# A chunked delta-rule attention ahead of two expert stages: state kept block-diagonal, keys and queries no longer spread, batch and token on the partitions, eight heads in one group

## The chip, the cores and the metric

The kernel runs on one core of a Trainium2 chip. The metric is the time of the device in microseconds for one execution; several runs give a median, and one further execution was recorded by the profiler. Five engines work side by side and meet through semaphores: TensorE (PE, matrix products into PSUM), VectorE (DVE), ScalarE (ACT), GpSimd (POOL) and SyncE (SP), which here issues DMAs. Each of them goes through its own instructions in order.

## The reference

Attention over 4 batches, 8 heads, 768 tokens and a head dimension of 48. Each head of each batch has a state of 48x48 that is carried from token to token:

```python
k_n = k / (np.linalg.norm(k, axis=-1, keepdims=True) + 1e-06)
for t in range(S):
    y[:, :, t] = np.einsum('bhd,bhde->bhe', q[:, :, t], state)
    v_old = np.einsum('bhde,bhd->bhe', state, kt)
    state = state + bt[:, :, :, None] * np.einsum('bhd,bhe->bhde', kt, vt - v_old)
```

Here kt, vt and bt are the normalised key, the value and beta of token t. The output, 3072 rows (batch and token) of 384, goes through a mixture of 8 experts of which each row takes the one with the highest logit, and the result through a second one of 4 experts that all rows pass, weighted by given probabilities. An expert is relu(x w1) w2 with 1024 hidden columns.

## The kernel before

**Attention in chunks.** 768 tokens are 24 steps of 32 tokens, `st = 4*c + s`, with six chunks c of four steps s. A step treats 32 tokens of 4 batches and 8 heads at once: 32 (batch, head) pairs. Within a step the recurrence is solved with a triangular matrix of 32x32 for each pair. `gram` (L311) multiplies keys with keys and with queries into G and Pm; `inverse` (L337) turns G into the inverse of the triangular matrix, all 32 x 4 matrices of a chunk at once: a transpose (L344), 31 columns, each with a product and a sum on DVE (L356, L357), and a transpose back (L380). The result goes as high and low fp16 halves into TPd, and by DMA (`stage_t`, L390) into the block-diagonal tiles TP of two steps each.

**A step.** `inject` (L406) puts v into a PSUM bank; `chain` (L411) subtracts state times keys (L424), writes the rest r as a high fp16 half on ACT and a low half on DVE, multiplies it with TP (L432) into u, again a high half (ACT) and a low half (DVE, L436), and adds keys times u to the state in PSUM (L444), whose two halves S go back to SBUF (ACT, and DVE L449) for the next step. Every product of two such numbers takes three matmuls (high-high, high-low, low-high). `outputs` (L453) computes the output from queries and state (L461) and from u and TP (L467); ACT copies it to ys, and the router's `done` (L539 on) normalises it, computes the expert logits and stores the rows (xr to xd). ACT's operations of this kind come from one helper and have its line, L203; DVE's and POOL's products of two tensors have L206.

**The form of the operands.** The tile kq holds the transposed keys and queries of a chunk (`keys`, L261: normalise, split, DMA transpose from l2, which lies in wa). It holds two (batch, head) pairs over its 128 partitions, 64 for each, and `spread` (L297) copies the keys (KT; DVE, some ACT) and queries (QT, ACT) of each step into zero-padded tiles, so that one matmul of 128 rows treats two pairs without mixing them. `stage_k` (L386) transposes the spread keys by DMA into kb for the state update. The eight heads are two groups g of four, with PSUM banks cp of their own, and each step runs chain and outputs for either.

**What sets the order.** Class `Plan` is a list scheduler: every operation is added with an assumed duration, the keys it reads and writes, and a priority; the plan starts the ready operation with the lowest priority on each engine, operations of `chain` being urgent, and emits all engines' instructions in the resulting order. `OFF` is a table of about 100 offsets to the priorities, by tag. SyncE issues the DMAs in order; a DMA also waits for the eighth one before it. Idle stretches of TensorE are filled with matmuls on zeros (L195). At the end of the attention `weights` loads the first experts' weights into the tiles kq, wa and wb. The first expert matmul is at L800.

## Time and profile before

| what | value |
|---|---|
| runs | 1446.67, 1441.14, 1443.97 us, median 1443.97 |
| profiled execution | 1452.08 us, span 1450.5 us |
| busy over the span | PE 89%, DVE 64%, ACT 48%, POOL 49% |
| chain that ended last, by engine | PE 50%, DVE 13%, DMA 11%, issue 11% |
| attention, to the first expert matmul | 472.05 us |

The shares of the whole span mix two different parts: the attention in the first third and the two expert stages behind it. Busy times of the attention alone are in the windows below. "Idle before" in a group of instructions is time in which the engine stood still just before one of them, and the name behind the arrow is what ended it.

### The profile page before, as it was taken

What the parts mean: (1) busy time and instruction counts of PE and PEld (TensorE: products, weight loads), DVE (VectorE), ACT (ScalarE), POOL (GpSimd) and SP (SyncE); (2) the same over time, 40 slices, a digit from 0 to 9 for tenths busy, and PEclk for the clock granted to TensorE, in tenths of its full rate; (3) what the DMA queues carried; (4) which work ended last, traced back from release to release, by engine and by line L of the source; (5) the groups of instructions that cost most, each with busy time, mean ns of one, the idle gap of its engine ahead of it and who ended that gap; (6) DMA issues with size and microseconds to landing.
All of it is one profiled execution on the core that took longest, in us unless ns stands there. A gap on an engine that the chain in (4) does not pass through costs nothing.

```text
span 1450.5 us, 35997 instructions
## 1 busy us (share of the span) xinstructions
PE 1289.6 (89%) x14904; PEld 1066.8 (74%) x14904; DVE 930.2 (64%) x1877; ACT 690.9 (48%) x1348; POOL 714.4 (49%) x927
## 2 busy tenths in 40 slices
PE   7677686777778798899989999999999999999997
PEld 4355475665566654455679999899998999999997
DVE  7979888859745556653285556855578555564654
ACT  2846464645464444542254444544445444444433
POOL 3445554533223478310185445744468444456664
PEclk8688878868889999999999999999999999999999
DMA  8968988794797786763220102101121011011200
GB/s 124 184 94 159 109 132 113 124 128 84 123 116 128 190 226 173 211 177 101 74 63 23 45 23 87 46 23 35 33 77 34 23 34 34 23 36 54 66 34 34
DMA packets 358888, 130.48 MB, mean 90 GB/s; under 512 B 314688, under 2 KB 348992, under 8 KB 358720
## 3 DMA queue, kind: packets, MB, share of 16 engines
q1 hardware_dynamic: 351856, 112.69, 40.4%
q0 software_dynamic: 6864, 15.45, 3.3%
q8 instruction: 118, 1.93, 0.6%
q14 instruction: 50, 0.41, 0.1%
HBM read 76.38 MB, written 14.96 MB: 63 GB/s over the span
## 4 chain that ended last, share of the span: by engine, by line
PE 50%; DVE 13%; DMA 11%; issue 11%; SPq 5%; POOL 5%; ACT 4%; another core or an unknown queue 0%; POOLq 0%; ACTq 0%; DVEq 0%
PE b L928 23%; PE b L947 20%; SPq L215 4%; DMA s<-in_moe_w_dram 4%; DMA TP<-TPd 4%; DVE tmp L356 2%; DMA kq<-wa 2%; PE b L800 1%; POOL q L775 1%; DVE KT L306 1%; POOL S L936 1%; DVE X L357 1%; DVE wa L357 1%; PE Sp L444 1%; DVE v L753 1%
## 5 line engine op out<-in xcount | busy, mean ns | idle before, releaser
L928 PE MATMUL b<-wb,v 128*128 128x256 f16 x3456 | 392.8, 273 | 0.3 <-ACT a L930 0.2
L928 PEld LDWEIGHTS <-v 128*128 128x128 f16 x3456 | 336.7, 98 | 37.9 <-issue 0.9
L947 PE MATMUL b<-v,h 128*128 128x192 f16 x4032 | 353.5, 247 | 11.6 <-DVE cc L955 6.4
L947 PEld LDWEIGHTS <-h 128*128 128x128 f16 x4032 | 338.7, 98 | 16.6 <-issue 8.6
L936 POOL TENSOR_TENSOR S<-a 128x256 f32<-128x256 f32 x192 | 149.7, 800 | 272.7 <-ACT a L930 272.5
L940 DVE TENSOR_TENSOR h<-a,h 128x768 f16<-128x768 f32 x96 | 135.0, 1407 | 145.8 <-ACT h L939 138.3
L940 DVE TENSOR_TENSOR h<-S,h 128x1024 f16<-128x1024 f32 x96 | 120.9, 1259 | 125.6 <-ACT h L939 125.6
L939 ACT ACTIVATE h<-S 128x1024 f16<-128x1024 f32 x96 | 101.4, 1056 | 199.5 <-POOL S L936 179.8
L930 ACT ACTIVATE a<-b 128x512 f32<-128x512 f32 x192 | 113.4, 594 | 143.8 <-PE b L928 134.8
L936 POOL TENSOR_TENSOR S<-S,a 128x256 f32<-128x256 f32 x96 | 133.8, 1394 | 0.0
L195 PE MATMUL wp<-wz 128*128 128x512 f16 x304 | 85.4, 424 | 10.1 <-DVE LG L556 7.4
L939 ACT ACTIVATE h<-a 128x768 f16<-128x768 f32 x96 | 80.8, 842 | 2.8
L936 POOL TENSOR_TENSOR S<-a,S 128x256 f32<-128x256 f32 x96 | 73.7, 768 | 7.2
L195 PEld LDWEIGHTS <-wz 128*128 128x128 f16 x398 | 40.6, 107 | 47.0 <-issue 18.0
L203 ACT ACTIVATE QT<-kq 64x512 f16<-64x512 f16 x96 | 60.0, 626 | 11.4 <-PE cp L461 6.5
L815 POOL DMA_DIRECT2D x<-y x27 | 19.7, 733 | 90.5 <-DVE y L813 80.8
L432 PE MATMUL cp<-r,TP 128*128 128x48 f16 x576 | 31.4, 198 | 36.8 <-DMA TP<-TPd 20.6
L803 DVE SCALAR_TENSOR_TENSOR h<-b,h 128x432 f16<-128x432 f32 (+2 forms) x72 | 39.6, 552 | 36.2 <-ACT h L802 35.3
L444 PE MATMUL Sp<-u,kb 64*128 64x48 f16 x1152 | 35.4, 193 | 29.4 <-DVE S L449 15.2
L955 DVE TENSOR_TENSOR cc<-b,sm 128x192 f32<-128x192 f32 x192 | 58.5, 345 | 3.1 <-ACT sm L952 3.1
L753 DVE SCALAR_TENSOR_TENSOR v<-s,v 128x512 f16<-128x512 f32 (+2 forms) x56 | 45.5, 840 | 23.0 <-ACT v L752 21.1
L550 POOL TENSOR_TENSOR ys<-ys,sc 128x384 f32<-128x384 f32 x24 | 20.9, 871 | 79.7 <-ACT xr L203 36.0
(249 smaller groups left out, 2145.6 us busy)
## 6 DMA issues: line engine op xcount, KB each, us to landing
wb<-x SPq DMA_DIRECT2D x72, 256.0 KB
...
```

Of the source, the lines that this page charges most:

```text
L195: nc.tensor.matmul(out=out,lhsT=wz[:,0:128],rhs=wz[:,0:out.shape[1]],start=start,stop=True,skip_group_check=True)
L203: self.op('A',dur,lambda: self.nc.scalar.activation(out=out,in_=in_,func=func,scale=scale),reads,writes,tag,**k)
L215: self.op(q,occ,(lambda: e.dma_start_transpose(out=out,in_=in_)) if turn else (lambda: e.dma_start(out=out,in_=in_)),reads,list(writes)+[( ...
L444: for a,b in ps: nc.tensor.matmul(out=Sp[:,pp,u],lhsT=kb[R,a,u],rhs=u16[R,b,u-o],start=(st,u,a,b)==(0,0,0,0),stop=last and b==1,skip_group ...
L753: self.op('V',69+1.042*n,lambda: self.nc.vector.scalar_tensor_tensor(out=lo,in0=s,scalar=64.0,in1=hi,op0=ALU.mult,op1=ALU.subtract),reads+ ...
L928: for c,y in PASS: nc.tensor.matmul(out=F[k][:,f],lhsT=w[:,c,d,c_:c_+128],rhs=self.xk[B%2][d][:,y,256*i:256*i+256],start=(f,z)==(0,0),stop ...
L930: self.op('A',620,lambda k=k,g=g: A.activation(out=a[ja][:,g].rearrange("p x t -> p (x t)"),in_=F[k].rearrange("p a t -> p (a t)"),func=AF ...
L936: self.op('G',750,lambda o=o,x=x,y=y,w=w: G.tensor_tensor(out=X[o],in0=X[x],in1=X[y],op=w),ka,[ks])
L939: self.op('A',200+.833*m,lambda h=h,q=q,g=g: A.activation(out=h[:,0,:,q],in_=g,func=AF.Copy),kg,[kh+(0,)])
L940: self.op('V',200+1.042*m,lambda h=h,q=q,g=g: V.tensor_tensor(out=h[:,1,:,q],in0=g,in1=h[:,0,:,q],op=ALU.subtract),kg+[kh+(0,)],[kh+(1,)])
L947: for z,(c,d) in enumerate(PASS): nc.tensor.matmul(out=Q[k][:,o,0:192],lhsT=h[:,c,g,x],rhs=w[:,d,m,y],start=(m,o,z)==(0,0,0),stop=(m,z)==( ...
L955: self.op('V',340,lambda o=o,k=k,y=y,x=x: V.tensor_tensor(out=o,in0=Q[k][:,y,0:192],in1=s[:,x],op=ALU.add),[('Q',k),('sm',z,x)],[ko])
```

## The change

The diff keeps the algorithm, its precision (high and low halves) and the expert stages, and lays out the attention in another way.

* k and q are no longer spread: the tiles KT and QT, `spread`, `stage_k`, `stage_q` and the DMA transposes into kb are gone. In their place the state is kept block-diagonal in S16, `[128, 2, 4, 4, 2, 48]`, zeroed once by POOL, and the products with it (`by_state`) are matmuls of 32 stationary columns, one for each batch, with 96 moving columns.
* The partition is batch and token. k and q are loaded in pieces of 32 tokens of one batch and 8 heads, 16 DMAs each for a chunk where there were 4 (8 of another shape for the first chunk); the first chunk's q comes over ACT's queue. l2k and l2q are tiles of their own, and kqT and l2k exist three times. The state update takes the keys straight from l2k, in matmuls of 32 rows, into four PSUM banks.
* The eight heads are one group: one bank c0 for v, r and the output, one bank c1 for u; r, u and the output are 128x384, S's halves 64x768 (two for each step and half).
* The gram's matmuls are 64 rows by 32 columns with 64 moving columns.
* `OFF` is empty, so priorities are those of the code. wa and wb are halves of one tile wab, the weights' claims stand in another order, NXR is 4, and the scale of the fp16 halves is 512 and 8 where it was 64 and 64.

```diff
-OFF = {'Ksp 1': 357.7, 'Ksp 2': -152.1, 'Ksp 5': 47.8, 'Qsp 10': 200.2,
...
+OFF = {}
...
-    RK,RQ,RT,RV=8,3,2,4
+    RT,RV,RB=2,4,3
...
+        self.kqT=[KQ(kq[:,0:8192]),KQ(wab[:,0:8192]),T("kqT2",[128,2,2,16,128],F16)]
+        self.l2k=[L2(kq[:,8192:12288]),L2(wab[:,8192:12288]),T("l2k2",[128,2,32,64],F16)]
+        self.l2q=T("l2q",[128,2,32,64],F16)
...
+        self.S16=[T(f"S16{i}",[128,2,4,4,2,D],F16) for i in range(2)]
...
+        self.Sp=Q("Sp",4); self.gp=Q("gp"); self.c0=Q("c0"); self.c1=Q("c1")
...
+        for i in range(2):
+            for l in range(2): self.op('G',900,lambda i=i,l=l: nc.gpsimd.memset(self.S16[i][:,l].rearrange("p a b x d -> p (a b x d)").bitcast(F32),0.0),(),[('S16',i,l,x) for x in range(2)],"zero")
...
-                self.dma(t.rearrange("p (h b) d -> p b h d",b=B)[:,b],h[b,t0:t0+128],(),[(n,b)],f"ld {c}",xfer=1090)
+                for s in range(4): self.dma(t[32*b:32*b+32,8*s:8*s+8],h[b,c,:,s],(),[(n,b,s)],f"ld {c}",xfer=270,occ=500,q='D' if c or n=='kf' else 'A')
...
+            for f in ff:
+                for x in range(2):
...
+                    gp=bank[:,0].rearrange("p (s u w i) -> p s u w i",s=2,u=4,w=2); R=slice(64*x,64*x+64)
+                    for s in range(2):
+                        def mm(s=s,f=f,w=w,gp=gp,R=R):
+                            for u in range(4):
+                                for a,b in self.HL:
+                                    for q in range(4):
+                                        T=slice(32*q,32*q+32); g=4*(2*f+s)+u
+                                        nc.tensor.matmul(out=gp[T,s,u,w[0]:w[-1]+1],lhsT=kqT[R,0,a,g,T],rhs=kqT[R,w[0]:w[-1]+1,b,g,T],start=(a,b)==(0,0),stop=b==1,skip_group_check=True)
...
-    def chain(self,st,g):
-        nc=self.nc; s=st%4; last=st==4*self.nsc-1
...
+    def by_state(self,out,w,st,ps,first=False):
+        s=st%4; t=self.kqT[st//4%self.RB][:,w]; S=self.S16[st%2]
+        for u in range(4):
+            for a,b in ps:
+                for q in range(4):
+                    T=slice(32*q,32*q+32)
+                    self.nc.tensor.matmul(out=out[T,0,96*u:96*u+96],lhsT=t[:,a,4*s+u,T],rhs=S[:,b,u,q].rearrange("p x d -> p (x d)"),start=first and (u,a,b)==(0,0,0),stop=b==1,skip_group_check=True)
...
+    def chain(self,st):
...
+            for x,ps in enumerate(HLP):
+                self.op('P',16*len(ps)*13,lambda ps=ps: self.by_state(self.c0,0,st,ps),[('kT',j),ko+(x,0),ko+(x,1)],['c0'],t,**U)
+        r16=self.r16
+        self.act(490,r16[:,0],rp,['c0'],[('r16',0)],t,scale=1.0/8,**U)
+        self.op('V',550,lambda: nc.vector.scalar_tensor_tensor(out=r16[:,1],in0=rp,scalar=1.0/8,in1=r16[:,0],op0=ALU.mult,op1=ALU.subtract),['c0',('r16',0)],[('r16',1)],t,**U)
...
+                for u in range(8):
+                    for a,b in ps: nc.tensor.matmul(out=up[:,u],lhsT=tp(a,u),rhs=r16[:,b,u],start=(u,a,b)==(0,0,0),stop=b==1,skip_group_check=True)
+            self.op('P',8*len(ps)*27,mm,self.TPk(st)+[('r16',x)],['c1'],t,**U)
...
+        l2=self.l2k[j]
+        for x,ps in enumerate(HLP):
             def mm(ps=ps):
-                for pp in range(2):
-                    R=slice(64*pp,64*pp+64)
-                    for u in us:
-                        for a,b in ps: nc.tensor.matmul(out=Sp[:,pp,u],lhsT=kb[R,a,u],rhs=u16[R,b,u-o],start=(st,u,a,b)==(0,0,0,0),stop=last and b==1,skip_group_check=True)
-            self.op('P',8*len(ps)*PEN,mm,[('kb',st%2),ku+(x,)],[('S',0),('S',1)],t,**U)
+                for u in range(4):
+                    for a,b in ps:
+                        for q in range(4):
+                            T=slice(32*q,32*q+32)
+                            nc.tensor.matmul(out=self.Sp[:,q,96*u:96*u+96],lhsT=l2[T,a,8*s+2*u:8*s+2*u+2].rearrange("p x d -> p (x d)"),rhs=u16[T,b,2*u:2*u+2].rearrange("p x d -> p (x d)"),start=(st,u,a,b)==(0,0,0,0),stop=last and b==1,skip_group_check=True)
+            self.op('P',16*len(ps)*13,mm,[('l2k',j,a,s) for a in range(2)]+[ku+(x,)],['S'],t,**U)
...
+        for x in range(2):
+            R=slice(64*x,64*x+64)
+            I=self.Sp[R,:,0:8*D].rearrange("p q (u x d) -> p x q u d",x=2,d=D)[:,x]; O=[Sn[R,l,:,:,x].rearrange("p u q d -> p q u d") for l in range(2)]
+            self.act(830,O[0],I,['S'],[kn+(0,x)],t,**U)
+            self.tt('V',950,O[1],I,O[0],ALU.subtract,['S',kn+(0,x)],[kn+(1,x)],t,**U)
...
+    def outputs(self,st):
...
+        if st>0: self.op('P',48*13,lambda: self.by_state(self.c0,1,st,self.HL,True),[('qT',j)]+[ko+(x,p) for x in range(2) for p in range(2)],['c0'],t)
+        def pu():
+            for u in range(8):
+                for a,b in self.HL: nc.tensor.matmul(out=yp[:,u],lhsT=tp(2+a,u),rhs=u16[:,b,u],start=(st,u,a,b)==(0,0,0,0),stop=b==1,skip_group_check=True)
+        self.op('P',24*27,pu,self.TPk(st)+[ku+(0,),ku+(1,)],['c0'],t)
+        self.act(490,self.ys[st%2],yp,['c0'],[('ys',st%2)],t,scale=-1.0/512)
...
-                if st+1<L: self.stage_k(st+1)
-                if st+2<L and s!=2 : self.stage_q(st+2)
-                for g in range(2): self.inject(st,g); self.chain(st,g)
-                for g in range(2): self.outputs(st,g)
+                self.inject(st); self.chain(st); self.outputs(st)
...
-    NXR=5
+    NXR=4
```

Three places of the order of instructions follow. Names with a number (r_120) are tiles of a round of buffers, and `x4` is so many alike in a row. First DVE in the middle of an inverse; before, it is that of a chunk in wb and wa:

```order
L356 TENSOR_TENSOR tmp<-wb,wa 128x247
L206 TENSOR_TENSOR r_120<-cp_140,r_120 128x192
L357 TENSOR_TENSOR wa<-wa,tmp 128x19x13
L540 TENSOR_SCALAR sc_156<-AM 128x1
L306 COPY KT_92<-kq 64x16x32
L356 TENSOR_TENSOR tmp<-wb,wa 128x252
L206 TENSOR_TENSOR r_121<-cp_142,r_121 128x192
L436 SCALAR_TENSOR_TENSOR u_123<-cp_141,u_123 128x192
L357 TENSOR_TENSOR wa<-wa,tmp 128x18x14
L306 COPY KT_92<-kq 64x16x32
L356 TENSOR_TENSOR tmp<-wb,wa 128x255
```

and in the changed kernel, in GX and X:

```order
L207 TENSOR_TENSOR S_116<-Sp,S_116 64x4x4x48 x2
L344 TENSOR_TENSOR X_105<-X_105,tmp 128x26x6
L494 TENSOR_REDUCE AM<-ys_119 128x1
L343 TENSOR_TENSOR tmp<-GX_103,X_105 128x175
L495 TENSOR_SCALAR sc_140<-AM 128x1
L271 TENSOR_REDUCE ss<-ksq_97 128x8
L344 TENSOR_TENSOR X_105<-X_105,tmp 128x25x7
L394 SCALAR_TENSOR_TENSOR r_113<-c_128,r_113 128x384
L343 TENSOR_TENSOR tmp<-GX_103,X_105 128x192
L271 TENSOR_REDUCE ss<-ksq_96 128x8
L344 TENSOR_TENSOR X_105<-X_105,tmp 128x24x8
```

Between the inverse's products and sums (tmp, then wa or X) the copies into KT are gone, and r, u and S come once for eight heads with twice the columns instead of once for each group.

SyncE around the first TP transfers of a chunk, before:

```order
L215 DMA_TRANSPOSE kb_114<-wb 128x16x128
L215 DMA v_119<-in_v_dram 32x8x48 x4
L215 DMA_TRANSPOSE kb_115<-wb 128x16x128
L215 DMA_TRANSPOSE kq<-wa 128x32x128
L215 DMA TP_98<-TPd 32x64x32 x4
L215 DMA xd<-xr_150 128x768
L215 DMA xd<-xr_151 128x768
L215 DMA TP_99<-TPd 32x64x32 x4
L215 DMA v_116<-in_v_dram 32x8x48 x3
L215 DMA qf<-in_q_dram 128x8x48 x4
L215 DMA_TRANSPOSE kq<-wa 128x32x128
L215 DMA v_117<-in_v_dram 32x8x48 x4
```

and in the changed kernel:

```order
L216 DMA bz<-in_beta_dram 128x1x32
L216 DMA kf<-in_k_dram 32x8x48 x4
L216 DMA v_112<-in_v_dram 32x8x48 x4
L216 DMA kf<-in_k_dram 32x8x48 x7
L216 DMA_TRANSPOSE wab<-l2q 128x32x128
L216 DMA TP_91<-TPd 32x64x32 x4
L216 DMA_TRANSPOSE wab<-wab 128x32x128
L216 DMA kf<-in_k_dram 32x8x48 x5
L216 DMA qf<-in_q_dram 32x8x48 x16
L216 DMA xd<-xr_137 128x768
L216 DMA v_109<-in_v_dram 32x8x48 x4
L216 DMA xd<-xr_138 128x768
```

The transposes into kb are gone; the pieces of kf and qf, 16 each for a chunk, stand ahead of and between the transposes and the TP transfers.

ACT at the start of the program, before:

```order
L230 ACT_TABLE_LOAD
L230 ACTIVATE s_106<-s_106 128x32
L203 ACTIVATE ksq_103<-kf 128x384
L203 ACTIVATE ksq_104<-kf 128x384
L203 ACTIVATE ksq_103<-kf 128x384
L203 ACTIVATE ksq_104<-kf 128x384
L203 ACTIVATE s_106<-ss 128x32
L203 ACTIVATE wa<-kf 128x8x48 x4
```

and in the changed kernel:

```order
L216 DMA qf<-in_q_dram 32x8x48 x2
L231 ACT_TABLE_LOAD
L231 ACTIVATE s_99<-s_99 128x32
L216 DMA qf<-in_q_dram 32x8x48 x13
L333 ACTIVATE X_105<-b_87 128x32
L216 DMA qf<-in_q_dram 32x8x48
L204 ACTIVATE l2q<-qf 128x8x48 x4
L204 ACTIVATE ksq_96<-kf 128x384
L204 ACTIVATE ksq_97<-kf 128x384
```

ACT issues the first chunk's 16 transfers of q and converts q before it squares the first keys (ksq).

## Rows read from the trace of the kernel before

**Rows 1.** Busy time of each engine in four stretches of the span: the stretch in us, its length, then for PE, weight loads, DVE, ACT and POOL the busy us and in brackets the instructions, then the granted TensorE clock as a share of full speed, the busy share of the DMA engines and GB/s.

```profile
0.00:39.20 39.20, 29.68 (x289) 15.91 (x289) 28.78 (x81) 10.71 (x24) 14.51 (x48) 0.86 0.82 132
39.20:404.30 365.10, 269.93 (x4947) 208.98 (x4948) 301.44 (x751) 213.58 (x531) 162.85 (x206) 0.80 0.83 126
404.30:472.00 67.70, 53.86 (x886) 42.34 (x886) 33.78 (x113) 34.69 (x88) 23.85 (x32) 0.85 0.83 111
472.00:1450.50 978.50, 936.17 (x8784) 799.59 (x8783) 566.17 (x935) 431.97 (x706) 513.17 (x643) 0.98 0.26 73
```

**Rows 2.** Timeline of DVE: start and duration in us, engine, line, operation. First and last instruction of the first inverse, first of the second, last of the sixth.

```profile
39.25 1.96 DVE L344 STREAM_TRANSPOSE wb<-GT 128x1024 f32<-128x1024 f32 x1
...
78.95 1.96 DVE L380 STREAM_TRANSPOSE wb<-wa 128x1024 f32<-128x1024 f32 x1
...
83.52 1.93 DVE L344 STREAM_TRANSPOSE GX<-GT 128x1024 f32<-128x1024 f32 x1 [0.62 <-POOL GT L206]
...
402.29 1.98 DVE L380 STREAM_TRANSPOSE GX<-X 128x1024 f32<-128x1024 f32 x1
```

**Rows 3.** Groups of DVE's instructions between 39.2 and 404.3 us: line, operation, tiles and shapes, count, then busy us and mean ns of one, then idle us before them with what ended it.

```profile
L356 DVE TENSOR_TENSOR tmp<-GX,X 128x112 f32<-128x112 f32 (+14 forms) x81 | 44.6, 551 | 1.2
...
L356 DVE TENSOR_TENSOR tmp<-wb,wa 128x112 f32<-128x112 f32 (+14 forms) x81 | 40.3, 497 | 1.3
...
L357 DVE TENSOR_TENSOR wa<-wa,tmp 128x112 f32<-128x112 f32 (+14 forms) x81 | 38.9, 481 | 1.3
...
L357 DVE TENSOR_TENSOR X<-X,tmp 128x112 f32<-128x112 f32 (+14 forms) x81 | 37.7, 466 | 1.3
...
L306 DVE COPY KT<-kq 64x512 f16<-64x512 f16 x48 | 25.9, 540 | 5.5 <-DMA kq<-wa 3.4 <-PE cp L432 1.2 <-PE cp L424 0.2
...
L449 DVE SCALAR_TENSOR_TENSOR S<-Sp,S 128x192 f16<-128x192 f32 x77 | 23.8, 350 | 11.9 <-ACT S L203 8.0 <-PE cp L424 2.1 <-PE cp L467 1.2
...
L436 DVE SCALAR_TENSOR_TENSOR u<-cp,u 128x192 f16<-128x192 f32 x39 | 13.5, 349 | 17.6 <-ACT u L203 17.0
...
L206 DVE TENSOR_TENSOR r<-cp,r 128x192 f16<-128x192 f32 x37 | 12.9, 348 | 11.6 <-ACT r L203 11.5
...
L306 DVE COPY wb<-kq 64x512 f16<-64x512 f16 x16 | 7.9, 496 | 1.3 <-DMA kq<-wa 1.1
```

**Rows 4.** Timeline of the start: start and duration in us, engine, line, operation, and in brackets the idle time before with what ended it. The first square on ACT, two of DVE's memsets, the first spread copies, and matmuls of the first chunk's gram.

```profile
4.35 0.52 ACT L203 ACTIVATE ksq<-kf 128x384 f32<-128x384 f32 x1 [1.91 <-DMA kf<-in_k_dram]
...
9.20 0.91 DVE L224 MEMSET TP<- 128x1024 f32 x1 [0.16 <-issue]
...
12.70 0.91 DVE L224 MEMSET QT<- 128x1024 f32 x1 [0.16 <-issue]
...
27.38 1.21 DVE L306 COPY wb<-kq 64x512 f16<-64x512 f16 x4 [3.12 <-DMA kq<-wa]
...
31.77 1.42 PE L327 MATMUL cp<-kq,wb 128*64 128x32 f16 x46 [0.42 <-DVE wb L306]
```

**Rows 5.** Instructions on SyncE's queue that issue the transfers of a tile: count, then shortest, median and longest issue in ns, and the us of the first and the last.

```profile
L215 SPq DMA_TRANSPOSE kb<-KT x18: 1626/2978/7843, 105.4 to 438.6; - x18
...
L215 SPq DMA_DIRECT2D v<-in_v_dram x96: 311/449/3211, 12.0 to 406.5; - x96
...
L215 SPq DMA_DIRECT2D kf<-in_k_dram x28: 384/588/2174, 0.9 to 199.0; - x28
...
L215 SPq DMA_DIRECT2D qf<-in_q_dram x28: 505/578/2951, 5.3 to 244.5; - x28
```

**Rows 6.** Groups of instructions by line, columns as in rows 3: three of ACT's (two of the attention, one of the expert stages) and one of DVE's at the start.

```profile
L203 ACT ACTIVATE QT<-kq 64x512 f16<-64x512 f16 x96 | 60.0, 626 | 11.4 <-PE cp L461 6.5 <-DMA kq<-wa 3.4
...
L203 ACT ACTIVATE xT<-wp 128x384 f32<-128x384 f32 x24 | 11.7, 488 | 5.6 <-PE wp L544 4.8 <-PE wp L195 0.7
...
L939 ACT ACTIVATE h<-a 128x768 f16<-128x768 f32 x96 | 80.8, 842 | 2.8
...
L290 DVE SCALAR_TENSOR_TENSOR wa<-qf,wa 128x384 f16<-128x384 f32 x4 | 2.0, 552 | 0.0
```

**Rows 7.** Timeline behind the last inverse: the hand-over of u from ACT to DVE, the first products with the last chunk's TP, and the last copy of the output.

```profile
407.01 0.32 ACT L203 ACTIVATE u<-cp 128x192 f16<-128x192 f32 x1
...
407.41 0.35 DVE L436 SCALAR_TENSOR_TENSOR u<-cp,u 128x192 f16<-128x192 f32 x1
...
418.26 1.12 PE L432 MATMUL cp<-r,TP 128*128 128x48 f16 x24 [2.38 <-DMA TP<-TPd]
...
463.16 0.66 ACT L203 ACTIVATE ys<-cp 64x192 f32<-64x192 f32 x2 [2.34 <-PE cp L467]
```

**Rows 8.** The chain that ended last, in order of time: start and duration in us, and what the time went to.

```profile
420.10 11.83 DMA kb<-KT
```

**Rows 9.** Timeline of TensorE in the fourth inverse's time: full-height products of 96 columns, and the gram's of 64 columns in tiles.

```profile
257.96 0.68 PE L461 MATMUL cp<-S,QT 128*128 128x96 f16 x12
...
259.13 0.95 PE L327 MATMUL gp<-kq,wb 128*64 128x64 f16 x48
```

**Rows 10.** Waits of the first 470 us: who waited, for what, then us in all, how often, and the longest.

```profile
ACT TPd L203 <- DMA TP<-TPd: 42.7, 8, 13.4
...
PE cp L432 <- DMA TP<-TPd: 20.6, 5, 8.8
...
ACT ksq L203 <- DMA kf<-in_k_dram: 8.2, 5, 4.3
```

More of the change, by code (lines that the diff above doesn't have):

```diff
@@ L282, in keys @@
         for i,q in enumerate(Q):
-            self.act(413,hi[:,q],kf[:,q],[('kn',i)],[('l2',0,i)],t)
-            self.tt(E,dE,lo[:,q],kf[:,q],hi[:,q],ALU.subtract,[('kn',i),('l2',0,i)]+([] if i<3 else kall),[('l2',1,i)],t)
-        turn(0)
-        t=f"keysq {c}"; qall=[('qf',b) for b in range(B)]
+            self.act(513,hi[:,q],kf[:,q],[('kn',i)],[n+(0,i)],t)
+            self.tt(E,dE,lo[:,q],kf[:,q],hi[:,q],ALU.subtract,[('kn',i),n+(0,i)]+kk('kf',i),[n+(1,i)],t)
+        turn(0,l2,[n+(x,q) for x in range(2) for q in range(4)])
@@ L295, in keys @@
-        turn(1)
-    def spread(self,st,w,tile,n,engs,t):
-        c,s=divmod(st,4); src,key=(self.kT,'kT') if w==0 else (self.qT[c%2],('qT',c%2)); slot=st%(self.RK if n=='KT' else self.RQ)
-        self.zero(tile,(n,slot),[(n,slot,l,h) for l in range(2) for h in range(2)],'V' if slot%2 else 'G')
-        for l in range(2):
-            for h in range(2):
-                R=slice(64*h,64*h+64); e=engs[2*l+h]
-                o=tile[R,l].rearrange("p u (a h i) -> p (u a) h i",h=2,i=32)[:,:,h]; i=src[R,l,:,32*s:32*s+32]
-                if e=='A': self.act(520,o,i,[key],[(n,slot,l,h)],t)
-                else: self.op('V',202,lambda o=o,i=i: self.nc.vector.tensor_copy(out=o,in_=i),[key],[(n,slot,l,h)],t)
@@ L378, in inverse @@
+        for j in range(31):
+            if j<28: upd('V',j,j+1,32,tmp,xd+[kxp],xd+[kxp,'tmp'])
+            else:
+                for i in range(j+1,32): self.op('V',160,lambda i=i,j=j: nc.vector.scalar_tensor_tensor(out=X[:,i,0:j+1],in0=X[:,j,0:j+1],scalar=GZ[:,j,i:i+1],in1=X[:,i,0:j+1],op0=ALU.mult,op1=ALU.add),[kg]+xd+[kxp]+([('xj',j,x) for x in range(j+1,31)] if i==31 else []),[('xj',j,i)]+(xd+[kxp] if i==31 else []),t)
         t=f"invT {c}"; self.prio+=0.5
@@ L400, in stage_t @@
             self.dma(tp[R,:,:,32*qq:32*qq+32].rearrange("p w u i -> p (w u) i"),self.TPd[R,f].rearrange("p w u i -> p (w u) i"),[('TPd',f,w) for w in range(4)],[('TP',sl,qq)],f"tp {st}",xfer=TPX)
-    def stage_q(self,st):
-        self.prio=st-2.5
-        self.spread(st,1,self.QT[st%self.RQ],'QT',SPQ,f"Qsp {st}")
     def TPk(self,st): return [('TP',st//2%self.RT,q) for q in range(4)]
-    def inject(self,st,g):
-        o=4*g; cp=self.cp[g][0][:,0]; v=self.v[st%self.RV][:,o:o+4].rearrange("p u d -> p (u d)"); self.prio=st-0.3
-        self.op('P',PV,lambda: self.nc.tensor.matmul(out=cp[:,0:4*D],lhsT=self.idv,rhs=v,start=True,stop=st==0,skip_group_check=True),['idv']+[('v',st%self.RV,b) for b in range(B)],[('cp',g,0)],f"inj {st} {g}")
@@ new lines, in inject @@
+    def inject(self,st):
+        v=self.v[st%self.RV].rearrange("p u d -> p (u d)"); self.prio=st-0.3
+        self.op('P',700,lambda: self.nc.tensor.matmul(out=self.c0[:,0,0:8*D],lhsT=self.idv,rhs=v,start=True,stop=st==0,skip_group_check=True),['idv']+[('v',st%self.RV,b) for b in range(B)],['c0'],f"inj {st}")
+    def by_state(self,out,w,st,ps,first=False):
[5 more added lines that the diff above has]
+                    self.nc.tensor.matmul(out=out[T,0,96*u:96*u+96],lhsT=t[:,a,4*s+u,T],rhs=S[:,b,u,q].rearrange("p x d -> p (x d)"),start=first and (u,a,b)==(0,0,0),stop=b==1,skip_group_check=True)
@@ L993, in deltanet_moe @@
             plan=Plan(tc,HOP)
[L994 removed]
+            at=Attention(c2,tc,plan,q,k,v,beta,r.kq,r.wab,r.done)
             at.prio=0; at.zs=set()
```

217 lines of the change are left out of this document (67 added, 150 removed).

## The prediction

> **What bounds the kernel now.** I read the windows by stage first [rows 1]. The attention takes 472 us of the span of 1450.5 us; the two expert stages behind it take 978.5 us with TensorE busy 936.2 us. The change leaves the expert stages' instructions alone, so they only move in time: all that can be won or lost lies before 472 us. In the attention no engine is busy through, but VectorE (DVE) comes nearest: 301.4 of 365.1 us between 39.2 and 404.3. The timeline of DVE says why that is the frame [rows 2]: the triangular inverse of a chunk begins with a transpose at L344 and ends with one at L380; the first begins at 39.25 and ends at 80.91, the second begins 2.6 us later, and the sixth ends at 404.27. So six inverses run nearly end to end on one engine and everything else of DVE's is squeezed between their operations. The groups by line show the shares [rows 3]: the four groups of the inverse's products and sums have 161.5 us (44.6+40.3+38.9+37.7); the copies that spread the keys (L306) 33.8; the low halves of state, u and r 50.2 (23.8+13.5+12.9). The idle 63.7 us go mostly to ACT's high halves (u 17.0, r 11.5, S 8.0). So the attention is three pieces in a row: a start (to 39.25), the six inverses (365), and a tail from 404.27 to 472: the last TP transfer, four steps and the router.
>
> **The change part by part.** The profiled execution took 1452.1 us, 8.1 above the median of the runs, 1443.97; I work on the first and subtract 8.1 at the end.
>
> Start. Today the first square of a key is at 4.35 us on ACT, behind a transfer of k [rows 4]. Now ACT issues the first chunk's 16 q transfers itself, and the four squares stand behind them and four conversions of q. ACT issuing a load is not in the trace; SyncE takes at least 505 ns for one of q's and 311 for one of v's [rows 5], so 16 are 5 to 8.1 us; I take 8.1, nearest in kind, and a first square near 10: +6. Against it, DVE has four 0.91 us memsets between 9.20 and 13.6 (first and last of them in [rows 4]) that keep the keys' scaling waiting; the zeroed spread tiles are gone and TP's are done while DVE would wait for q: -3.5. The gram of the first chunk begins at 27.38 with a copy and ends at 39.25, 11.9 us. Its k half becomes 384 matmuls of 32 columns without copies; 46 took 1.42 us here, 27 ns each behind a first one of 0.18, so 10.4 us and a product, 10.9: -1. Sum +1.5, taken as **+2**, with bounds -4 (the issues overlap the wait for k) and +6 (nothing given back).
>
> Inverses. Of DVE's work the 64 copies go: -33.8. The low halves change shape. A 128x192 one takes 350 ns [rows 3], one of 128x384 552 [rows 6], so 1.05 ns for a column more, and 64x768 comes to 955 by the same slope. In the window there were 77, 39 and 37 of S, u and r; now half as many: 38.5 x 0.955 + 19.5 x 0.552 + 18.5 x 0.552 = 57.8, +7.6. (S's new form reads four banks in a strided order, which no row shows: between 0.55, the time of half its columns, and 1.40, four times 350 for its four banks; that is -15 to +17 over all.) The inverse's own operations don't change. Busy time falls by 26. The idle time is the open half. The waits on ACT should halve in number and lengthen (0.49 us for 128x384 [rows 6] instead of 0.33); 6.8 us before L306 go with the copies [rows 3]. Against that, the table of offsets that set the order is emptied and loads come in more pieces. I let these cancel: idle as now, **-26**. Bounds on the idle: -35, if the engine loses over half of its gaps, and +45, if the inverses are spaced by late loads (below).
>
> What lies beside them costs nothing while the inverses cover it: ACT loses all copies of q to spread form (60.0 us of QT [rows 6]), SyncE 24 transposes kb at 2.98 us of issue in the larger group [rows 5], and TensorE gets twice the gram's matmuls (384 instead of 192 a chunk). It also gets 24 x 48 columns for u times TP instead of 24 x 96.
>
> Tail. From 404.27 the transfer of TP lasts until the first product at 418.26, 14.0 us, which I leave; four steps end with the copy of ys at 463.82 [rows 7], 45.6 us, and in them 11.83 us of the chain wait for kb [rows 8], a transfer that no longer exists. One step in the new form, along its longest path: state's high half 0.84 (a 128x768 conversion [rows 6]) and two low halves of 0.955, the first beside the second high half: 2.75; last key products 16 at 16 ns and 0.18, 0.44; r 0.49+0.55; the second half of TP times r, 8 at 47 ns [rows 7], 0.37; u 1.04; the last update products 0.44; nine hand-overs of 0.08 (ACT's u ends at 407.33, DVE's begins at 407.41 [rows 7]) 0.7: 6.8. One bank c0 now serves v, r and the output, so the next step's injection waits for the copy to ys: up to 1. With some 0.6 for the router's conversions in between, 8.4, four times 33.6: **-12**. Bounds: 0 (both groups' overlap is missed as much as the kb wait is worth) and -18 (no loss on c0, shorter TP wait). The 8.2 us of router behind it stay.
>
> Narrow tiles: the gram's 48 matmuls of 64 rows by 64 columns took 0.95 us at 16 ns each, while full-height ones of 96 columns took 44 ns [rows 9]; the former can only be so quick if neighbouring tiles overlap. I take the same for the new tiles of 32 columns or 32 rows. The Trainium skill, page "TensorEngine Tiling (Array Packing)", section "Key Properties", says that changing the tiling mode, rather than the tile, drains TensorE, and "Gotcha 2: Feature Incompatibilities" that column tiling loses the fast weight load; the kernel now goes from 32-column to full to 32-row tiles in each step, which speaks against the change. No row here shows either mode; by that page the step would lengthen as the third rival does.
>
> Sum: 2 - 26 - 12 = -36: 1416 profiled, **1408** as a median.
>
> **The rivals.**
> *More goes than the work.* DMA is busy 0.83 in the window [rows 1]; 24 transposes leave it. ACT waited 42.7 us for TP's transfers and TensorE 20.6 [rows 10]; were half of the larger to come off the inverses' spacing and a third of the tail's 14 us, another 26 goes: about 1382. For it: those waits hold ACT's whole queue, and u, r and S stand behind it. Against: loads come in four times as many pieces.
> *The order takes it back.* The idle grows by what the busy time lost, since the offsets had placed exactly these waits; the tail gains, the start loses and a little slips there too: -36 + 26 + 7, 1441. For it: the DVE idle is made of hand-overs, not of missing work. Against: the inverses in the new order stand back to back as well, with less between them.
> *Tiles do not overlap.* 48 products at 44 ns are 2.1 us instead of 0.8, twice on a step's path: +2.6. Under the inverses that is hidden; in the tail it is 10.4, and some gram time at the start adds 6: 1424.
> *Slower: the loads in pieces.* A chunk's k and q come in 32 transfers instead of 8. At 0.45 to 0.59 us of issue [rows 5] that is 14 to 19 us on SyncE, in order, where today 4.7 are spent. The TP transfers, the transposes and v stand between or behind them, and ACT's squares wait for k (8.2 us today [rows 10]) ahead of r, u and S in ACT's order. If each of five chunks is late by 11 us, that is +55, against the kernel's -36: +19, 1463. It decides from about 7 us a chunk, where the gain is used up. For it: the pieces stand ahead of the third chunk's first TP transfers in SyncE's order. Against: loads are placed one to two chunks ahead, and 24 transposes of nearly 3 us, 70 us of issue, leave the same queue.
>
> **How the numbers follow.** Forecast (1390 to 1437) 0.48; more goes 0.17; tiles 0.05; order takes it back 0.11; loads in pieces 0.19. A measurement of this kernel can tell about 0.5%, 7.2 us, from no change. Faster is the first three, 0.70; same 0.11; slower 0.19. All terms at their low bounds give -4 - 76 - 18, -98, and at their high ones +6 + 36 + 0, +42 (the strided S included); neither is likely in all parts. The range 1376 to 1460 leaves out the far end of the second case and most of the last one; the forecast's own is 1390 to 1437.
>
> **What would show it.** Right: in the new profile the first transpose of GT near 41 us, the last transpose of an inverse near 380, the tail's four steps near 34 us, the first expert matmul (L800 before) near 436, DVE busy about 275 us between first and last inverse, and S's low half near 0.95 us. Wrong: inverses spaced over 68 us apart with DVE idle before L344 or ACT waiting for kf (loads in pieces); r and u of a step spread far apart with nothing missing (the order); runs of 48 products near 2 us (tiles); a tail step over 11 us (the single bank c0).

## The result: 1% slower, 14 us

The changed kernel takes 1456.46 us (median, 1455.4 to 1465.98) beside 1442.56 for the kernel before: a ratio of 1.0107, 95% interval 1.0058 to 1.0155. A second set of runs gave 1.0098 (1.0067 to 1.0129). The prediction was 1408, with a chance of 0.19 for slower; it is wrong in sign and outside the forecast's own range of 1390 to 1437; the outer range, 1376 to 1460, just holds it.

### The profile page after: what moved, and what is told of

The parts are those of the page before. It is cut to its first block, busy times and chain, and to the rows that moved or that the text cites. A ratio compares the mean times of both kernels' runs of the same rounds, so it can differ in the third digit from the quotient of the medians.

```text
span 1453.8 us, 40181 instructions
## 1 busy us (share of the span) xinstructions
PE 1294.8 (89%) x17187; PEld 1034.4 (71%) x17187; DVE 904.3 (62%) x1699; ACT 612.2 (42%) x1070; POOL 714.7 (49%) x927
## 4 chain that ended last, share of the span: by engine, by line
PE 49%; DMA 12%; issue 12%; DVE 10%; SPq 7%; POOL 6%; ACT 2%; POOLq 0%; ACTq 0%; DVEq 0%
PE b L882 22%; PE b L901 20%; SPq L216 6%; DMA s<-in_moe_w_dram 4%; DMA TP<-TPd 2%; DMA qf<-in_q_dram 2%; DVE X L344 2%; DVE tmp L343 2%; POOL q L729 2%; POOL S L890 1%; PE wp L196 1%; PE c L382 1%; DVE v L707 1%; DMA xt<-xg 1%; DVE h L894 1%
## 5 line engine op out<-in xcount | busy, mean ns | idle before, releaser
L882 PE MATMUL b<-wab,v 128*128 128x256 f16 x3456 | 392.7, 273 | 0.1
L196 PE MATMUL wp<-wz 128*128 128x512 f16 x570 | 157.1, 423 | 6.6 <-DVE LG L511 5.0
L196 PEld LDWEIGHTS <-wz 128*128 128x128 f16 x833 | 76.0, 106 | 77.7 <-issue 26.5
L344 DVE TENSOR_TENSOR X<-X,tmp 128x60 f32<-128x60 f32 (+8 forms) x162 | 81.7, 504 | 3.0
L343 DVE TENSOR_TENSOR tmp<-GX,X 128x60 f32<-128x60 f32 (+8 forms) x162 | 79.9, 493 | 2.9
L757 DVE SCALAR_TENSOR_TENSOR h<-b,h 128x432 f16<-128x432 f32 (+2 forms) x72 | 39.6, 553 | 29.0 <-ACT h L756 28.6
L207 DVE TENSOR_TENSOR S<-Sp,S 64x768 f16<-64x768 f32 x46 | 43.9, 953 | 21.4 <-ACT S L204 16.7
```

The source lines that it names most:

```text
L196: nc.tensor.matmul(out=out,lhsT=wz[:,0:128],rhs=wz[:,0:out.shape[1]],start=start,stop=True,skip_group_check=True)
L343: self.op(e,d,lambda: eng.tensor_tensor(out=tm,in0=a.to_broadcast(sh),in1=X[:,j:j+1,0:j+1].to_broadcast(sh),op=ALU.mult),[kg]+reads,[tk],t)
L344: self.op(e,d,lambda: eng.tensor_tensor(out=X[:,r0:r1,0:j+1],in0=X[:,r0:r1,0:j+1],in1=tm,op=ALU.add),[tk],writes,t)
L882: for c,y in PASS: nc.tensor.matmul(out=F[k][:,f],lhsT=w[:,c,d,c_:c_+128],rhs=self.xk[B%2][d][:,y,256*i:256*i+256],start=(f,z)==(0,0),stop ...
```

## The profile after

The profiled execution took 1455.4 us. Windows of the changed kernel at the same four stages as [rows 1] (columns as there):

```profile
0.00:42.73 42.73, 27.64 (x574) 14.27 (x576) 18.20 (x46) 9.92 (x21) 12.71 (x47) 0.83 0.69 122
42.73:422.72 379.99, 284.78 (x6961) 189.19 (x6946) 289.27 (x637) 150.62 (x308) 166.19 (x210) 0.82 0.61 95
422.72:482.06 59.34, 47.88 (x897) 31.81 (x895) 28.77 (x86) 19.52 (x35) 20.67 (x28) 0.88 0.62 85
482.06:1453.80 971.74, 934.51 (x8784) 799.11 (x8783) 568.07 (x934) 432.14 (x706) 515.15 (x643) 0.99 0.26 74
```

The start is 3.5 us longer, the tail 8.4 shorter, and the six inverses, for which 26 us less were forecast, take 15 us more: the attention ends at 482.06 instead of 472.05. The expert stages, whose instructions are the same, took 971.7 us here and 978.5 in the profile of before; in the profiles of the experiments below they take 969 to 978 in either layout. So this pair of profiles shows less of the loss than the medians do.

Groups of DVE's instructions between first and last inverse (columns as in [rows 3], whose groups they answer):

```profile
L344 DVE TENSOR_TENSOR X<-X,tmp 128x60 f32<-128x60 f32 (+8 forms) x162 | 81.7, 504 | 3.0
L343 DVE TENSOR_TENSOR tmp<-GX,X 128x60 f32<-128x60 f32 (+8 forms) x162 | 79.9, 493 | 2.9
L207 DVE TENSOR_TENSOR S<-Sp,S 64x768 f16<-64x768 f32 x40 | 38.1, 953 | 15.8 <-ACT S L204 11.1 <-PE gp L315 3.8 <-issue 0.6
...
L394 DVE SCALAR_TENSOR_TENSOR r<-c,r 128x384 f16<-128x384 f32 x21 | 11.7, 557 | 19.9 <-ACT r L204 19.6
...
L402 DVE SCALAR_TENSOR_TENSOR u<-c,u 128x384 f16<-128x384 f32 x20 | 11.0, 550 | 18.4 <-ACT u L204 18.4
L494 DVE TENSOR_REDUCE AM<-ys 128x1 f32<-128x384 f32 x20 | 10.9, 547 | 11.9 <-ACT ys L204 11.6 <-POOL l2q L207 0.3
...
L511 DVE TENSOR_SCALAR LG<-wp 128x16 f32<-128x16 f32 x19 | 3.2, 167 | 8.2 <-PE wp L509 6.7 <-PE wp L196 1.5
```

and two groups of the kernel before that belong beside the last two (the maximum of ys, and the expert logits LG):

```profile
L539 DVE TENSOR_REDUCE AM<-ys 128x1 f32<-128x384 f32 x18 | 9.8, 546 | 2.4 <-ACT ys L203 2.2 <-POOL Pm L206 0.2
...
L556 DVE TENSOR_SCALAR LG<-wp 128x16 f32<-128x16 f32 x18 | 3.0, 164 | 1.4 <-PE wp L195 0.8 <-PE wp L554 0.6
```

The inverse's two groups have 161.6 us where four had 161.5, and the new low halves last what was worked out: 953, 557 and 550 ns. What grew is the idle time: 379.99 - 289.27 = 90.7 us against 63.6 of before, in front of the maximum of ys (2.4 to 11.9), r (11.6 to 19.9), the logits (1.4 to 8.2) and S (11.9 to 15.8). In front of the logits DVE waits for TensorE, in front of the others mostly for ACT. The busy time fell by 12.1 us (301.4 to 289.3), not by the 26 forecast. TensorE's timeline shows something that the kernel before has in one run of matmuls only, for 1.7 and 1.2 us: it stands still inside a run of matmuls for "issue", that is with nothing waited for. Places of 1 us and more in the changed kernel (start, duration, operation, and in brackets the idle time before it):

```profile
37.31 0.46 PE L315 MATMUL c<-kq 64*32 64x32 f16 x37 [2.30 <-issue]
...
41.04 0.22 PE L315 MATMUL gp<-kq 64*32 64x32 f16 x5 [2.48 <-issue]
...
45.32 0.24 PE L315 MATMUL gp<-kq 64*32 64x32 f16 x9 [2.12 <-issue]
...
49.32 0.46 PE L315 MATMUL c<-kq 64*32 64x32 f16 x37 [2.73 <-issue]
...
194.81 0.29 PE L315 MATMUL gp<-kq 64*32 64x64 f16 x6 [7.43 <-issue]
...
257.73 0.88 PE L315 MATMUL gp<-wab 64*32 64x64 f16 x50 [4.38 <-issue]
```

There are 13 such places between 30 and 425 us, 32 us together. From the first gap to the second lie 37 + 91 = 128 matmuls, each with a weight load, and 5 + 48 + 75 = 128 more to the third.

At 174 us the other suspect, the loads in pieces, is seen as well. SyncE, then TensorE, ACT and DVE:

```profile
174.72 11.05 SPq L216 DMA_DIRECT2D qf<-in_q_dram  x15
...
186.37 6.58 SPq L216 DMA_DIRECT2D v<-in_v_dram  x4
...
196.46 4.68 SPq L216 DMA_DIRECT2D TP<-TPd  x3
```

```profile
196.60 1.15 PE L382 MATMUL c<-S,wab 128*32 128x96 f16 x48
```

```profile
192.73 0.52 ACT L204 ACTIVATE qf<-qf 128x384 f32<-128x384 f32 x1 [6.28 <-issue]
196.08 0.52 ACT L204 ACTIVATE qf<-qf 128x384 f32<-128x384 f32 x1 [2.83 <-DMA qf<-in_q_dram]
...
197.81 0.49 ACT L204 ACTIVATE r<-c 128x384 f16<-128x384 f32 x1 [0.43 <-PE c L382]
```

```profile
198.33 0.56 DVE L394 SCALAR_TENSOR_TENSOR r<-c,r 128x384 f16<-128x384 f32 x1 [9.50 <-ACT r L204]
```

Fifteen pieces of q occupy SyncE for 11 us ahead of v and TP, ACT stands 6.3 us for nothing that the profile shows and then waits 2.8 us for q, with r queued behind, and DVE stands for 9.5 us, the longest of its waits for r. But r's own last wait is for TensorE's product with the state (L382, at 196.60), which stands behind the gap of 7.43 us that ends at 194.81. So this stall has both suspects in it, and TensorE's path is the one that ends last. In gram_hi (below), where the gram has no gap here, r goes as soon as ACT has its q, and DVE waits 5.7 us.

## The experiments

Ratios are to the kernel before, measured beside each of them on the same chip. Stages are in us from the one profile of each kernel; the two profiles of the changed kernel differ by some 3 us in the inverses and 2 in the tail, so a difference of that size says little; "idle" is DVE's between first and last inverse, "gaps" TensorE's issue gaps of 1 us and more between 30 and 425 us, count and sum. The diffs show only the changed part of a line.

| kernel | ratio (95%) | start | inverses | tail | idle | gaps |
|---|---|---|---|---|---|---|
| before | 1 | 39.3 | 365.0 | 67.8 | 63.6 | 2, 2.9 |
| changed | 1.0107 (1.0058-1.0155) | 42.7 | 380.0 | 59.3 | 90.7 | 13, 32 |
| before_no_table | 0.9923 (0.9895-0.9951) | 39.6 | 352.7 | 59.1 | 55.5 | none |
| order_searched | 0.9993 (0.9958-1.0027) | 43.4 | 368.4 | 58.6 | 83.4 | 14, 26 |
| no_k_loads | 1.0072 (1.0043-1.0102) | 41.7 | 377.7 | 57.6 | 88.2 | 13, 30 |
| more_loads | 1.0543 (1.0467-1.0618) | 54.7 | 435.0 | 59.1 | 152.7 | 10, 24 |
| q_on_act | 1.0115 (1.0072-1.0158) | 49.9 | 376.5 | 57.2 | 85.1 | 13, 25 |
| q_on_act_no_k | 1.0065 (1.0043-1.0087) | 49.2 | 368.6 | 63.6 | 76.7 | 10, 26 |
| q_on_act_searched | 1.0033 (1.0002-1.0063) | 50.1 | 364.1 | 62.6 | 79.5 | 17, 35 |
| before_searched | 0.9836 (0.9790-0.9883) | 39.2 | 353.3 | 58.3 | 57.3 | 1, 2.4 |
| gram_hi | 1.0014 (0.9990-1.0037) | 42.2 | 366.5 | 61.0 | 75.6 | 4, 7 |
| gram_hi_no_k | 0.9919 (0.9895-0.9944) | 34.7 | 363.8 | 63.5 | 72.4 | 4, 10 |
| before_gram_twice | 0.9939 (0.9906-0.9973) | 43.5 | 354.1 | 56.8 | 67.7 | 8, 13 |
| measured_durations | 1.0287 (1.0238-1.0336) | 49.4 | 385.3 | 63.8 | 98.3 | 8, 24 |
| measured_searched | 1.0172 (1.0116-1.0228) | 46.1 | 381.4 | 63.3 | 100.9 | 10, 22 |
| before_measured_searched | 1.0135 (1.0077-1.0192) | 39.5 | 394.2 | 54.4 | 93.5 | 1, 1.7 |
| searched_gram_hi | 0.9904 (0.9869-0.9938) | 41.9 | 345.5 | 58.9 | 56.2 | 4, 9 |
| gram_narrow | 1.0098 (1.0063-1.0134) | 42.9 | 379.3 | 58.6 | 88.3 | 13, 30 |
| after_again | 1.0098 (1.0067-1.0129) | 42.6 | 382.8 | 57.0 | 94.6 | 11, 30 |

### Order against loads

```diff
-OFF = {'Ksp 1': 357.7, 'Ksp 2': -152.1, 'Ksp 5': 47.8, 'Qsp 10': 200.2,
...
+OFF = {}
```

> The kernel before with its table of priority offsets emptied, nothing else. Theory O (order): what the layout won was given back because the offsets that had placed the waits are gone; then the old layout loses the same way, by 20 to 45 us: 1463 to 1488. Theory L (loads in pieces): the order hardly matters, the 32 pieces a chunk on SyncE do; then this kernel, which has the large loads, stays within 10 us of 1443.

It went the other way: 0.9923 (1426.2, outside theory L's range as well). The table had cost the old layout 11 us, so its emptying is no loss of the change. Against this kernel, which shares the empty table, the new layout alone is 1.0107 / 0.9923 = 1.0185, some 27 us slower. The windows of before_no_table:

```profile
0.00:39.64 39.64, 29.82 (x291) 15.56 (x291) 28.98 (x76) 10.60 (x24) 14.53 (x48) 0.88 0.92 143
39.64:392.38 352.74, 273.80 (x5129) 211.19 (x5130) 297.25 (x783) 223.23 (x554) 167.31 (x218) 0.84 0.84 133
392.38:451.52 59.14, 44.05 (x731) 33.70 (x729) 25.00 (x87) 24.01 (x64) 15.92 (x21) 0.86 0.74 102
```

DVE is busy 8 us more there than in the changed kernel, and idle 35 us less.

```diff
-OFF = {}
+OFF = {'pr': 153.5, 'invT 4': 178.3, 'ldv 4': -178.4,
...
```

> The changed kernel with a new table of offsets, found by a random search against the planner's own durations; same instructions of the attention, other order. Theory O: DVE's idle time between the inverses falls from 90.7 towards the 63.7 us of before, and the time to 1415 to 1435. Theory L: the pieces are still there, so not below 1448.

0.9993: 16 us came back, from the inverses (368.4); the idle time fell to 83.4, far from 63.6, and the time, 1442.3, reached neither range. Order has a share, and not all.

```diff
+HALF = ('ld 1','ld 2','ld 3','ld 4','ld 5')
...
+w_=list(writes)
...
-(lambda: e.dma_start(out=out,in_=in_))
+(lambda: None) if tag in HALF and w_[0][0]=='kf' else (lambda: e.dma_start(out=out,in_=in_))
```

> The changed kernel in the same order, without the 16 loads of k for each of the chunks 1 to 5 (the first chunk's keys are used again, so the output is another): 80 of the 176 pieces on SyncE are gone, about 36 us of issue. Theory L: half of the lateness goes, 15 to 25 us: 1432 to 1442. Theory O: only the direct waits of ACT for k (7 us between the inverses, some more at the start) go: 1448 to 1456.

```diff
+HALF = ('ld 1','ld 2','ld 3','ld 4','ld 5')
...
-(lambda: e.dma_start(out=out,in_=in_))
+(lambda: [e.dma_start(out=out[:,4*x:4*x+4],in_=in_[:,4*x:4*x+4]) for x in range(2)]) if tag in HALF else (lambda: e.dma_start(out=out,in_=in_))
```

> The changed kernel in the same order, each piece of k and q of the chunks 1 to 5 issued as two halves of four heads: 64 loads a chunk instead of 32, some 14 us more of issue on SyncE a chunk. Theory L: +25 to +55 us, 1480 to 1510. Theory O: at most +10, 1456 to 1466.

The two answers look unlike each other. Taking 80 pieces away brought 5 us (1450.7, in theory O's range, and the intervals overlap), adding 160 cost 63 (1521.1, above theory L's range): about the 72 us of issue that 160 pieces of 0.45 us take. So SyncE's queue seems to have a little room at 32 pieces a chunk and none at 64: theory L is right at double the number and not at the number that the change has.

### Are q's pieces in the way?

```diff
-q='D' if c or n=='kf' else 'A'
+q='D' if n=='kf' else 'A'
```

> The changed kernel with the q pieces of all chunks issued by ACT, as those of the first chunk are; 80 of 160 pieces leave SyncE's queue, ACT gets some 16 x 0.5 us a chunk. So far: doubling the pieces cost 64 us in the same order, leaving out half of them (k) gave back 5.8. Theory Q (SyncE's queue is just full: q's pieces stand in front of TP's transfers and hold ACT and through it DVE): the 9.5 us stall of DVE at 198 us and its like go, 1430 to 1445. Theory G (one group: with a single chain nothing stands between the hand-overs of r, u and S): little changes, 1450 to 1460.

> The kernel with q's pieces on ACT, in the same order, and besides without the 80 loads of k for the chunks 1 to 5 (the first chunk's keys are used again, so the output is another): no piece of k or q is left on SyncE after the first chunk. Theory Q: 1420 to 1435, and DVE's idle time between first and last inverse below 70 us. Theory G: not below 1442, idle above 80 us.

> q's pieces on ACT and a table of offsets searched for this kernel against the planner's own durations. The search brought 14 us to the changed kernel; if pieces and order are separate losses the gains add: 1418 to 1432. If they are the same loss, 1435 to 1445.

q_on_act gives 1.0115 (1460.5, at the end of theory G's range). Its inverses are 3.5 us shorter, and its start is 7 us longer, as the second chunk's q now stands in ACT's queue. With k's loads out too the inverses take 368.6 and the time, 1453.1, is in theory G's range, the idle time (76.7) between the two. Pieces on SyncE are then worth some 11 us of the inverses, not the loss, and 6 us of the time (1.0065). The searched table is worth 12 us here: 1.0033 (1449.4), above both ranges.

> The kernel before with a table searched in the same way. Emptying its table alone gave 1426. If the search is worth here what it was worth there (14 us), 1408 to 1418; if the planner's durations carry no information about the chip, 1420 to 1435.

0.9836. The median, 1423.3, lies in the second range; by the ratios the search is worth 0.9923 - 0.9836, 12.5 us, near the 14 of the first expectation. So the same search does nearly as much for the old layout as for the new one (16 us), and with a searched table in both the new one is still 0.9993 / 0.9836 = 1.016, some 23 us slower. before_searched is the fastest kernel of this study, 1423.28 us, 1.6% below the kernel before and 2.7% below the changed one; its edit is again the table alone.

### Too many instructions for TensorE

```diff
-                                for a,b in self.HL:
+                                for a,b in self.HL[:1]:
...
-start=(a,b)==(0,0),stop=b==1
+start=(a,b)==(0,0),stop=True
```

> The changed kernel in the same order, with only the first (high times high) of the gram's three products: 128 matmuls a chunk instead of 384, 256 the first chunk instead of 768; the gram is less precise. The changed kernel's TensorE stands still some 31 us between first and last inverse for nothing but issue, in gaps of 1.3 to 7.4 us inside runs of small matmuls, the kernel before with its table emptied nowhere. Theory I (instructions: TensorE goes through its narrow matmuls faster than its instructions arrive): those gaps fall below 12 us and the time to 1432 to 1444. Theory G (one group, hand-overs): 1450 to 1457.

> The changed kernel in the same order with both: only the gram's first product, and no loads of k for the chunks 1 to 5 (other keys, another output). If instructions and pieces are separate losses: 5 to 6 us below gram_hi. If the pieces were what delayed the instructions: as gram_hi, within 3 us.

gram_hi: 1.0014, 13 us gained; the gaps fell from 32 to 7 us, as theory I said, and the inverses to 366.5. The time, 1448.0, lies between the two ranges. With k's loads out as well: 0.9919. That is 14 us below gram_hi, not 5. The two profiles are 7.8 us apart, and 7.6 of that lie in the start:

```profile
0.00:42.24 42.24, 25.13 (x287) 11.82 (x289) 18.02 (x47) 10.02 (x21) 12.71 (x47) 0.84 0.69 124
42.24:408.74 366.50, 279.64 (x5454) 177.76 (x5442) 290.89 (x637) 150.12 (x308) 166.57 (x210) 0.81 0.61 98
```

```profile
0.00:34.65 34.65, 26.24 (x287) 12.09 (x289) 17.77 (x46) 9.91 (x22) 12.73 (x47) 0.94 0.74 132
34.65:398.43 363.78, 269.61 (x5459) 171.40 (x5446) 291.37 (x637) 149.94 (x308) 167.43 (x210) 0.84 0.56 90
```

The first fence is gram_hi, the second gram_hi_no_k. Each of the two edits alone leaves the first inverse at 42 us, and both bring it to 34.65. So two things hold the start side by side: the gaps in the first chunk's 768 gram matmuls (the first two stand in the 384 of k, which the inverse needs), and the squares of the second chunk's keys, which wait for its pieces (ACT's first stands 18.3 us for k in gram_hi, until 39.79) and whose sums are queued on DVE ahead of the first inverse. In the inverses the two edits add: 13.5 and 2.3 us alone, 16.2 together. At 0.9919 the new layout is where the old one is with its table emptied (0.9923), though it does less than that: a third of the gram's products, and no loads of k behind the first chunk.

```diff
-for a,b in self.HL: nc.tensor.matmul(out=gp[R,u]
+for a,b in self.HL*2: nc.tensor.matmul(out=gp[R,u]
```

> The kernel before with its table emptied (1426) and every product of the gram issued twice (the second pass starts the sum anew, so the output is the same): 384 matmuls a chunk as in the changed kernel, in the same order. Theory I: issue gaps appear in the gram's runs on TensorE, and the time grows by 8 to 25 us: 1434 to 1451. Theory G: within 5 us of 1426.

Half a miss. The gaps appear in the old layout too once the gram has as many matmuls, 8 of them, 13 us together, for example

```profile
42.56 0.30 PE L327 MATMUL gp<-kq,KT 128*64 128x32 f16 x3 [3.10 <-issue]
```

and the start grows by 4 us, but the ratio, 0.9939, can't be told from 0.9923. From this gap to the next, and from that to the third, lie 128 matmuls each, as in the changed kernel. So gaps alone don't make the loss. DVE's idle time did grow by 12 us (55.5 to 67.7), but its busy time fell by 11 (297.3 to 286.4) with as many instructions; why it fell is not shown.

gram_hi takes away instructions and work at once. This run separates them:

```diff
-nc.tensor.matmul(out=gp[T,s,u,w[0]:w[-1]+1],lhsT=kqT[R,0,a,g,T],rhs=kqT[R,w[0]:w[-1]+1,b,g,T],
+n=32 if (a,b)==(0,0) else 4; nc.tensor.matmul(out=gp[T,s,u,w[0]:w[-1]+1,0:n],lhsT=kqT[R,0,a,g,T],rhs=kqT[R,w[0]:w[-1]+1,b,g,32*q:32*q+n],
```

> The changed kernel in the same order; the gram's second and third products are issued as before (384 matmuls a chunk) but take only the first 4 of 32 columns of each block, so the gram is less precise. It tells apart why leaving those matmuls out gave 13 us. Theory I (their number: TensorE's instructions arrive too slowly): nothing is won, ratio 1.006 to 1.013, and the issue gaps of some 31 us between 35 and 425 us stay. Theory W (their work: fewer columns through the array): most is won, ratio 0.999 to 1.004.

> The changed kernel as it is, for its ratio to the kernel before on the same chip as gram_narrow: 1.0107 again, 1.006 to 1.015.

1.0098 for both, to the last digit. The gaps are where they were, after the same counts, though two thirds of the gram's matmuls have 4 columns:

```profile
37.80 0.44 PE L315 MATMUL c<-kq 64*32 64x4 f16 x37 [2.51 <-issue]
...
41.80 0.20 PE L315 MATMUL gp<-kq 64*32 64x4 f16 x5 [2.77 <-issue]
```

It is the number of TensorE's instructions that costs these 13 us, not the columns in them. That it costs them by way of the gaps is argued from the traces: the matmuls left out took some 10 ns each besides. The Trainium skill, "Runtime: NRT & Kernel Launch", section "Instruction fetch mechanics", says that instructions arrive in blocks of 256 and that this is mostly hidden. The distance agrees (128 matmuls with their weight loads); hidden it is not where matmuls stand 10 ns apart. No run shows the arrival of instructions itself.

### Order again

```diff
-            d=n/0.96+68 if e=='V' else n/0.48+68
+            d=1.7*(n/0.96+68) if e=='V' else n/0.48+68
...
-48*(9 if c else 18)
+48*28
...
-16*len(ps)*13
+16*len(ps)*28
...
-48*13
+48*28
```

> The changed kernel with its table empty, and two of the planner's durations set to what the trace shows: the inverse's operations 1.7 times as long (planned 268 ns on average, measured 498) and the narrow matmuls at 28 ns each instead of 9 or 13 (a block of 128 of them is followed by a gap). Only the order changes. Theory P (the order is made on wrong times, so VectorE's in-order queue waits at r, u and S): the idle time of VectorE between first and last inverse falls from 90.7 to below 72, ratio to the kernel before 0.985 to 0.998. Theory G (one chain: the waits are inherent): ratio 1.003 to 1.013.

> The same with a table of offsets searched against these durations. Theory P: the search is worth more with true durations than with the old ones (ratio 0.9993): 0.975 to 0.990. Theory G: 0.993 to 1.003.

> The kernel before with the inverse's planned durations 1.7 times as long and a table searched against them; the search on the old durations gave 0.9836. Theory P: also better, 0.970 to 0.982. Theory G says nothing of it; 0.98 to 0.99 if the planner's durations don't matter.

All three are misses for theory P, and outside theory G's ranges too: 1.0287, 1.0172 and 1.0135, with idle times of 93 to 101 us. The gaps are no more than with the planner's own durations (8, 10 and 1). Durations nearer to the mean of the trace made a worse order in both layouts.

> The changed kernel with the first searched table (ratio 0.9993) and only the first product of the gram (which gave 1.0014 alone); same order as with that table, the gram less precise. If order and instructions are separate losses the ratio is 0.988 to 0.992; if the search had only moved the same stalls, 0.996 to 1.001.

0.9904. Order and instructions are separate losses and add. Its windows:

```profile
0.00:41.91 41.91, 26.02 (x325) 12.36 (x325) 18.82 (x48) 9.81 (x21) 13.01 (x47) 0.85 0.70 125
41.91:387.42 345.51, 255.56 (x5142) 169.06 (x5136) 289.26 (x629) 145.62 (x298) 165.99 (x208) 0.80 0.65 103
```

The idle time is 345.51 - 289.26 = 56.2 us with all 32 pieces a chunk and a single chain of eight heads. That rules out theory G in its strong form: the single chain does not force the waits. By the ratios the kernel before with its searched table (0.9836) is still 10 us faster; no run accounts for those.

## Why the prediction was wrong, point by point

- **What bounds.** Right: the six inverses on DVE are the frame before and after, and the time was decided there.
- **DVE's work, -26.** Half right. Between first and last inverse, where the term stands, DVE is busy 289.3 us, not the 275 forecast: -12.1. The sizes of the new low halves were right to 1%, and the copies' 33.8 us are gone; but the low halves took 10.6 us more than before instead of 7.6, as more steps fell between the inverses, the expert weights' conversions there (L617, now L571) rose from 8.3 to 11.8 us, which leaves -20; why the busy time fell by 12 only is not shown. Over the attention's three stages DVE's work fell by 27.8 us (364.0 to 336.2), but 10.6 of that lie in the start and 5.0 in the tail.
- **"I let these cancel: idle as now."** This is the step that failed. Idle rose by 27 us and more than took back the work: -12 and +27 make the inverses' +15. The runs put the number of TensorE's instructions in its place for about half: with the gram's extra instructions out, 15 us of idle and 13 us of the time go, and DVE's waits for ACT fall in front of r (19.6 to 12.1) and u (18.4 to 9.8), though not of S. The order has a share, a smaller one than its gain suggests: a searched table takes 16 us off the time, and 19 us off the idle once the gram is cut (75.6 to 56.2), but the old layout wins 12.5 us by such a search as well. I had costed the doubled number of gram matmuls at nothing, under the inverses' cover; DVE's cover doesn't hold for the engine that DVE waits for.
- **The start, +2.** 3.5 came, for other reasons. The first square is at 13.9 us, later than the 10 forecast, but what sets the start are the gram's gaps and the second chunk's keys, neither of which was a term.
- **The tail, -12.** -8.4: right in sign, a third short. The steps are better than worked out, 30.0 us from the first product (446.20) to the last copy of ys (476.19) instead of 33.6; but the first product comes 23.5 us after the last inverse, not 14.0: SyncE is 21.5 us over the eight TP transfers.

```profile
425.98 21.53 SPq L216 DMA_DIRECT2D TP<-TPd  x8
```

- **Rival: loads in pieces (0.19).** Right in the sign and near in the time, 1463, for mostly another reason, so the nearness is luck: k's pieces cost 2 us in the inverses and k's and q's together 11, where it had 55, 11 for each of five chunks. Its point of decision was not far: doubled, they cost 55 us in the inverses and 12 in the start.
- **Rival: the order takes it back (0.11).** Its mechanism, the emptied table, has the wrong sign: the old layout gained 11 us from it. That this new order is poor is shown by order_searched, and that the old one's was as well by before_searched.
- **Rival: more goes than the work (0.17).** Wrong: the DMA engines' busy share in the inverses did fall (0.83 to 0.61), but the inverses grew longer.
- **Rival: tiles do not overlap (0.05).** Wrong:

```profile
209.70 0.35 PE L411 MATMUL Sp<-u,wab 32*128 32x96 f16 x16
209.98 0.78 PE L428 MATMUL c<-u,TP 128*128 128x48 f16 x24
210.69 0.95 PE L315 MATMUL gp<-kq 64*32 64x64 f16 x96
```

From 32-row tiles to full height to 64x32 tiles there is no pause, and the gram's 96 take 10 ns each. The caution from the Trainium skill, "TensorEngine Tiling (Array Packing)", section "Key Properties", that a change of mode drains TensorE, doesn't show as a cost here. [rows 9] had been misread: its gram matmuls, `128*64`, are 128 rows by 64 columns, so they were column tiles already, and no row there had 64 rows.

What stays open: why the planner's order is poor in either layout, since truer mean durations made it worse; the 10 us between the two layouts that are left with searched tables and the gram cut; and the part of the single chain, of which only the strong form is ruled out. Two chains in the new layout were not tried, as all eight PSUM banks are taken.
